# Q's parity copies by DMA, twenty more B1 blocks inside attention, and the second norm's apply on GpSimd

## The chip, the cores and the metric

The kernel runs on one core of a Trainium2 chip. The metric is the device time in microseconds (us) of one execution, the median of several runs. The engines are named as in the profile: PE is TensorE (PEld its weight loads), DVE is VectorE, ACT is ScalarE, POOL is GpSimd, SP is SyncE, which here issues every DMA.

## The reference

One block of a transformer with conditioning, in bf16, with S = 2048 tokens, D = 512 features, 32 heads of 16, a window of 256 keys, and F = 1792.

```python
mod = (silu(c) @ w_mod).reshape(1, 6, 1, 512)       # sa, ca, ga, sb, cb, gb
h = layernorm(x) * (1 + ca) + sa
x = x + ga * A(h)      # q, k, v = h @ wqkv; softmax over the last 256 keys; @ wo
h = layernorm(x) * (1 + cb) + sb
x = x + gb * B(h)

def B(x):              # a token-mixing MLP: it contracts over the 2048 tokens
    h = layernorm(x)
    u = gelu(einsum('bsd,sf->bdf', h, w1) + b1)     # "B1"
    y = einsum('bdf,fs->bds', u, w2) + b2           # "B2"
    return y.transpose(0, 2, 1)
```

Between the two halves each token thus passes a second norm with a scale and a shift (its result is called h2 in the kernel) and a third norm without them (its result is hb, the input of B1).

## The kernel before, in words

Tokens are worked in 16 blocks of 128 (`tb`, also `sc` where B1 contracts over them) and in 4 groups of 4 blocks (`tg`). Heads are worked in 4 groups of 8 (`g8`). Everything between startup and the tail is one stage, called attention here, whose order is written out by hand under `tc.manual_schedule()`: what is emitted first on an engine runs first on it.

**Units.** Attention is a loop over 80 units (`units`): 4 token groups x 4 head groups x 5 kinds (`KINDS`). Each unit has its scores on PE into PSUM (`emit_scores`, L548, L555, L575, L585), two exponentials of 128x1024 on ACT (`emit_exp`, L598), and its products with V on PE (`av_a` L609, `av_c` L623). After units 2 and 4 of a head group the product leaves PSUM by a transpose on DVE (`norm_out`, L655). When both have left, `norm_rest` divides: a reciprocal on DVE (L666), a multiply on POOL that writes `merge` (L667), and a transpose back on DVE that writes `OTd` (L675).

**Dense groups.** Each unit can also carry one dense group: four times four matmuls of 128x32 columns (`dense`, L271) into the single PSUM tile `dn`, and its eviction on DVE. `plan` lays out which: the projections Q, K and V of this token group and of the next (`qk_group`, `v_group`), the transposes of the next group's normalised tokens (`transpose_group`, L253), the output projection `wo_group` of the previous group's tokens (its eviction, L370, adds to x), and, in the last group, `part_group`: B1 blocks for the columns `fc` in `PART`, over the token blocks that are ready, accumulated in PSUM and kept as `part` in SBUF. A tail loop starts those columns at `sc` = 8. Groups 1 and 2 have a dense group in all units but 16 and 19, group 3 in all but 11.

**Q by parity.** Scores of even and of odd heads use the same rows of K, so Q is kept twice, `QT[:, 0]` with the odd heads' rows at zero and `QT[:, 1]` with the even heads' rows at zero. `qk_group` evicts Q to `qs` on DVE (L309), and POOL multiplies it by the two masks (L313).

**Second and third norm.** `ln23` follows each output projection in three steps: p1 takes statistics of x (DVE L683 and L685; then POOL L204 and L208 for one over the root), p2 applies them on DVE (L695) and scales and shifts on POOL (L699, L700), p3 takes statistics of h2 and applies them on POOL (L214 and L215, `apply_by_pool`) into `hb`. These steps, the divisions and the first norm of the next group wait in lists (`chains`); `fill` emits a step when a planner's clock of DVE and POOL says that there is room. So the planned costs set the order on DVE and POOL. At most LIVE = 4 token blocks are between p2 and p3.

**DMAs.** SP issues them in order. In attention these are `copies_for` (L633: the pieces of V for the unit kind "C", for the first head group at unit 0, for the others at units 3, 4 and 5), and in group 1 the first NA = 10 of 16 blocks of w1, half a block a unit, each paced behind an exponential (L408). The other blocks of w1 (`w1b`) and w2 are loaded when attention has ended.

**Tail.** PE runs B1 for the columns 0 to 5 over `sc` 0 and 1, then the output projection of the last four blocks (`t_wo`, L986, which reads all four `OTd[3]`), interleaved with `sc` 2 and 3; then `sc` 4 to 15 (L964); then the other columns in pairs (L1050), their gelu (`emit_gelu`, which first adds `part` on DVE, L973, for the columns that have it), and B2 (L1086) with its result.

Of the kernel before, what the change touches and what calls it, by code (L numbers as in the profile page):

```python
# [8 lines left out]
DT = mybir.dt  # L9
ACT = mybir.ActivationFunctionType  # L10
ALU = mybir.AluOpType
# [10 lines left out]
NF = F // P  # L22
EPS = 1e-5
SCORE_SCALE = DH ** -0.5
NA = 10
LIVE = 4
SLACK = 0.3

# [2 lines left out]
def kernel(  # L31
# [59 lines left out]
    hbpool = ctx.enter_context(tc.tile_pool(name="hbpool", bufs=1))  # L91
    hb = [hbpool.tile([P, D], DT.bfloat16, name=f"hb_{t}") for t in range(NT)]
    opool = ctx.enter_context(tc.tile_pool(name="opool", bufs=2))

    PART = (6, 7, 8, 9)
    ppool = ctx.enter_context(tc.tile_pool(name="ppool", bufs=1))
    part = {fc: ppool.tile([P, D], DT.float32, name=f"part{fc}") for fc in PART}
    wqpool = tc.alloc_tile_pool(name="wqpool", bufs=1)
# [66 lines left out]
    build_masks()  # L165


    qpool = tc.alloc_tile_pool(name="qpool", bufs=2)
    kpool = tc.alloc_tile_pool(name="kpool", bufs=1)
    vpool = tc.alloc_tile_pool(name="vpool", bufs=1)  # L170
    qspool = tc.alloc_tile_pool(name="qspool", bufs=2)
# [21 lines left out]
    nc.gpsimd.memset(ones[:], 1.0)  # L193


    for tg in range(NG):
        VaugT[tg] = Vring[tg % 2]
        for g8 in range(ND):
            KT[tg][g8] = Kring[tg % 2][:, g8, :]

# [91 lines left out]
    def qk_group(tg, g8, kind, pool):  # L292
        col0 = g8 * P + (D if kind == "k" else 0)

        def mms():
            pq = pool.tile([P, 4 * P], DT.float32, name="dn")
            for dc in range(ND):
                dense(
                    pq, lhsT=wqkv[:, dc, col0 : col0 + P], rhs=h1T[tg][:, dc, :],
                    start=(dc == 0), stop=(dc == ND - 1),  # L300
                )
            return pq

        def evac(pq):
            if kind == "k":
                nc.vector.tensor_copy(out=KT[tg][g8], in_=pq[:])  # L306
                return
            qs = qspool.tile([P, 4 * P], DT.bfloat16, name="qs")
            nc.vector.tensor_copy(out=qs[:], in_=pq[:])  # L309
            QT[tg][g8] = qpool.tile([P, 2, 4 * P], DT.bfloat16, name=f"QT{g8}")  # L310
            for n, m in enumerate((mask_even, mask_odd)):
                eng = nc.vector if (tg, g8, n) == (0, 1, 0) else nc.gpsimd
                eng.tensor_scalar(  # L313
                    out=QT[tg][g8][:, n, :], in0=qs[:], scalar1=m[:], scalar2=0.0, op0=ALU.mult, op1=ALU.add,
                )
            return 0.7 if (tg, g8) == (0, 1) else 1.4
        return mms, evac, (1.05 if (tg, g8, kind) == (0, 1, "q") else 0.7)
# [70 lines left out]
    with tc.manual_schedule():  # L388
# [116 lines left out]
        for dc in (0, 2, 1, 3):  # L505
            for ps, col0 in ((pq, 0), (pk, D)):
# [1 line left out]
                    ps, lhsT=wqkv[:, dc, col0 : col0 + P], rhs=h1T[0][:, dc, :],  # L508
                    start=(dc == 0), stop=(dc == ND - 1),
                )  # L510
        QT[0][0] = qpool.tile([P, 2, 4 * P], DT.bfloat16, name="QT0")

        def q_half(n, m, lo, hi):
            nc.vector.tensor_scalar(
# [145 lines left out]
        def norm_rest(tg, g8):  # L660
            t2v = state["t2"][:].rearrange("p a (b c) -> p a b c", c=32)
            m = npool.tile([P, 4 * P], DT.bfloat16, name="merge")

            def quotient():
                zr = npool.tile([P, 2, 16, 1], DT.float32, name="zr")
                nc.vector.reciprocal(out=zr[:], in_=t2v[:, :, :, DH : DH + 1])  # L666
                nc.gpsimd.tensor_tensor(  # L667
                    out=m[:].rearrange("p (b a d) -> p a b d", a=2, d=DH), in0=t2v[:, :, :, 0:DH],
                    in1=zr[:].to_broadcast([P, 2, 16, DH]), op=ALU.mult,
                )  # L670
                return 1.06

            def back():
                OTd[tg][g8] = opool.tile([P, 4 * P], DT.bfloat16, name=f"OTd{g8}")
                nc.vector.transpose(out=OTd[tg][g8][:], in_=m[:])  # L675
            return [(quotient, 0.36), (back, 0.72)]

        def ln23(tb):
            v = {}

            def stats(src, key):
                st = small.tile([P, nc.vector.BN_STATS_DIM], DT.float32, name="ln2_stats")
                nc.vector.bn_stats(out=st[:], in_=src)  # L683
                v[key] = small.tile([P, nc.vector.BN_AGGR_DIM], DT.float32, name="ln2_mv")
                nc.vector.bn_aggr(out=v[key][:], in_=st[:])  # L685
                v[key + "r"] = rstd_of(v[key][:, 1:2], 1, "ln2")

            def p1():
                stats(xres[tb][:], "m2")
                return 0.85  # L690

            def p2():
                live.add(tb)
                h2 = v["h2"] = lnpool.tile([P, D], DT.bfloat16, name="h2")
                nc.vector.tensor_scalar(  # L695
                    out=h2[:], in0=xres[tb][:], scalar1=v["m2"][:, 0:1], scalar2=v["m2r"][:],
                    op0=ALU.subtract, op1=ALU.mult,
                )
                nc.gpsimd.tensor_tensor(out=h2[:], in0=h2[:], in1=bc_cb1, op=ALU.mult)  # L699
                nc.gpsimd.tensor_tensor(out=h2[:], in0=h2[:], in1=bc_sb, op=ALU.add)  # L700
                return 2.4

            def p3():
                stats(v["h2"][:], "m3")
                apply_by_pool(hb[tb][:], v["h2"][:], v["m3"][:, 0:1], v["m3r"][:])
                done.add(tb)
                live.discard(tb)
                return 2.0
            return [(p1, 0.8), (p2, 0.37, lambda: len(live) < LIVE), (p3, 0.8)]

        chains = []
        live = set()
# [25 lines left out]


        def part_group(fc, k):  # L740
            def mms():
                assert done >= set(range(4 * k, 4 * k + 4))
                if k == 0:
                    part[fc, "ps"] = ps_dn.tile([P, D], DT.float32, name="dn")
                for sc in range(4 * k, 4 * k + 4):
                    dense(
                        part[fc, "ps"], lhsT=w1box["a"][:, sc, fc * P : (fc + 1) * P], rhs=hb[sc][:],
                        start=(sc == 0), stop=(sc == 7),
                    )
                return part[fc, "ps"]  # L750

            def evac(ps):
                if k == 1:
                    nc.vector.tensor_copy(out=part[fc][:], in_=ps[:])
            return mms, evac, 0.7 * k


        wo_next = iter(range(12))
# [1 line left out]
        def plan(tg):  # L760
            at, then = {}, {}

            def lay(ul, group):
                assert ul not in at, (tg, ul)
                at[ul] = group

            def qk(ul, g, g8, kind):
                lay(ul, qk_group(g, g8, kind, ps_dn))

            for n in (2, 3):  # L770
                lay(n - 2, v_group(tg, n, ps_dn))
            if tg == 0:
                for ul, g8, kind in ((2, 1, "q"), (3, 1, "k"), (4, 2, "q"), (5, 2, "k"), (6, 3, "q"), (7, 3, "k")):
                    qk(ul, tg, g8, kind)
                lay(8, bias_group(ps_dn))
                lay(13, bc_group(ps_dn))
                then[18] = [(lambda g=g: fold_wod(g), 0.0) for g in range(ND)]
            else:
                for ul, g8, kind in ((2, 1, "k"), (3, 2, "q"), (4, 2, "k"), (5, 3, "q"), (8, 3, "k")):
                    qk(ul, tg, g8, kind)  # L780
                for ul in (6, 7, 9, 10):
                    tb = next(wo_next)
                    lay(ul, wo_group(tb, ps_dn))
                    then[ul] = ln23(tb)
            if tg + 1 < NG:
                t0, t1, q0, v0, k0, q1, v1 = (10, 11, 12, 16, 14, 15, 18) if tg == 0 else (11, 12, 13, 14, 15, 17, 18)
                lay(t0, transpose_group(tg + 1, 0, ps_dn))
                lay(t1, transpose_group(tg + 1, 1, ps_dn))
                lay(v0, v_group(tg + 1, 0, ps_dn))
                lay(v1, v_group(tg + 1, 1, ps_dn))  # L790
                for ul, g8, kind in ((q0, 0, "q"), (k0, 0, "k"), (q1, 1, "q")):
                    qk(ul, tg + 1, g8, kind)
            else:
                for n, fc in enumerate(PART):
                    for k in range(2):
                        lay(12 + 2 * n + k, part_group(fc, k))
            return at, then
# [235 lines left out]
    with tc.tile_pool(name="gtmp", bufs=2) as gtmp:  # L1033
# [9 lines left out]
        for n, fg in enumerate(fgroups[2:]):  # L1043
            pu = ps_u[n % 2].tile([P, 2, D], DT.float32, name=f"pu{n % 2}")
            for sc in range(NT):
                for i, fc in enumerate(fg):
                    s0 = 8 if fc in PART else 0
                    if sc < s0:
                        continue
                    nc.tensor.matmul(  # L1050
                        pu[:, i, :], lhsT=w1_of(sc, fc), rhs=hb[sc][:],
                        start=(sc == s0), stop=(sc == NT - 1),
                    )
            for i, fc in enumerate(fg):
                emit_gelu(pu, i, fc, gtmp)
# [67 lines left out]
```

## Time and profile before

| what | value |
|---|---|
| runs | 267.12, 264.77, 265.92 us; median 265.92 |
| profiled execution | 264.77 us, of which the span from first to last instruction is 263.0 |
| granted TensorE clock, mean | 0.993 |
| PE busy | 240.8 us (92%) |
| DVE busy | 167.2 us (64%) |
| ACT busy | 164.3 us (62%) |
| POOL busy | 128.6 us (49%) |
| first and last exponential start | 13.6 and 164.2 us |
| chain that ended last | PE 70%, DVE 18%, ACT 5%, issue 3%, DMA 2% |

The shares are averages over three stages: startup to 13.6 us, attention to about 166 us, and the tail. In attention PE, ACT, DVE and POOL all work; in the tail it is PE, with DVE and ACT for gelu and the result. A line of a group reads: source line, engine, operation, out<-in with shapes, count, then busy us and mean ns of one, then the idle time of its engine before it and what ended that.

### The profile page before, as it was taken

What the parts mean: (1) busy time and instruction counts of PE and PEld (TensorE: products, weight loads), DVE (VectorE), ACT (ScalarE), POOL (GpSimd) and SP (SyncE); (2) the same over time, 40 slices, a digit from 0 to 9 for tenths busy, and PEclk for the clock granted to TensorE, in tenths of its full rate; (3) what the DMA queues carried; (4) which work ended last, traced back from release to release, by engine and by line L of the source; (5) the groups of instructions that cost most, each with busy time, mean ns of one, the idle gap of its engine ahead of it and who ended that gap; (6) DMA issues with size and microseconds to landing.
All of it is one profiled execution on the core that took longest, in us unless ns stands there. A gap on an engine that the chain in (4) does not pass through costs nothing.

```text
span 263.0 us, 11079 instructions
## 1 busy us (share of the span) xinstructions
PE 240.8 (92%) x4923; PEld 129.6 (49%) x4933; DVE 167.2 (64%) x353; ACT 164.3 (62%) x193; POOL 128.6 (49%) x218
## 2 busy tenths in 40 slices
PE   6988798899998879989899899999999999999994
PEld 2544455455555545555456455444444444444443
DVE  6678868875798697898786877789411001423444
ACT  6688998999999989999999999100082110000000
POOL 6104943699269998898995498954200000000000
PEclk9999979999999999999999999999999999999999
DMA  5949962134744342000122000999800000202021
GB/s 168 340 143 250 245 215 79 47 89 123 224 130 133 110 129 73 6 2 5 32 75 53 5 2 24 333 417 414 356 3 0 2 0 0 80 2 80 20 101 40
DMA packets 26084, 29.95 MB, mean 114 GB/s; under 512 B 3252, under 2 KB 23476, under 8 KB 26036
## 3 DMA queue, kind: packets, MB, share of 16 engines
q1 hardware_dynamic: 26036, 29.25, 35.4%
q8 instruction: 38, 0.62, 1.0%
q14 instruction: 10, 0.08, 0.1%
HBM read 22.55 MB, written 2.23 MB: 94 GB/s over the span
## 4 chain that ended last, share of the span: by engine, by line
PE 70%; DVE 18%; ACT 5%; issue 3%; DMA 2%; SPq 1%; ACTq 0%; DVEq 0%
PE dn L271 19%; PE py L1086 18%; PE pu L1050 8%; PE pu L964 7%; PE pss L548 5%; ACT et L598 5%; PE po L609 4%; PE po L623 3%; DVE t L655 3%; DVE qs L309 3%; DVE VaugT L287 2%; DMA wmod<-in_w_mod_dram 2%; PE pss L555 2%; DVE KT L306 2%; DVE x L370 1%
## 5 line engine op out<-in xcount | busy, mean ns | idle before, releaser
L598 ACT ACTIVATE et<-pss 128x1024 bf16<-128x1024 f32 (+1 forms) x160 | 143.8, 995 | 6.4 <-PE pss L555 5.1
L1086 PE MATMUL py<-guT,w2r 128*128 128x512 bf16 (+1 forms) x234 | 48.3, 366 | 0.2
L1065 DVE SCALAR_TENSOR_TENSOR o<-py,bFM,bc 128x512 bf16<-128x512 f32 (+1 forms) x17 | 11.7, 715 | 44.4 <-PE py L1086 44.4
L271 PE MATMUL dn<-h1T,wqkv 128*32 128x512 bf16 x496 | 33.1, 381 | 3.9 <-DVE VaugT L287 1.3
L1086 PEld LDWEIGHTS <-w2r 128*128 128x128 bf16 x238 | 23.3, 98 | 25.3
L548 PE MATMUL pss<-QT,KT 32*128 32x64 bf16 (+2 forms) x704 | 28.9, 238 | 5.8 <-ACT et L598 4.8
L655 DVE STREAM_TRANSPOSE t<-po 128x512 f32<-128x512 f32 x32 | 22.8, 711 | 11.4 <-PE po L623 11.2
L208 POOL TENSOR_TENSOR ln_rstd<-ln_ve,mhalf 128x1 f32<-128x1 f32 (+1 forms) x40 | 24.1, 602 | 5.7 <-DVE ln_ve L204 2.6
L204 POOL TENSOR_SCALAR ln_ve<-ln_mv 128x1 f32<-128x1 f32 (+1 forms) x38 | 9.1, 240 | 34.7 <-DVE ln_mv L226 17.6
L548 PEld LDWEIGHTS <-KT 32*128 32x128 bf16 x704 | 15.4, 92 | 21.3 <-issue 11.1
L609 PE MATMUL po<-et,VaugT 128*32 128x64 bf16 (+2 forms) x704 | 25.1, 241 | 0.0
L609 PEld LDWEIGHTS <-VaugT 128*32 128x32 bf16 x704 | 17.2, 96 | 11.0 <-issue 2.1
L271 PEld LDWEIGHTS <-wqkv 128*32 128x32 bf16 x512 | 13.1, 95 | 13.5 <-issue 6.0
L555 PE MATMUL pss<-mask_q,mask_k 32*128 32x256 bf16 (+1 forms) x256 | 19.2, 263 | 0.0
L667 POOL TENSOR_TENSOR merge<-t,zr 128x512 bf16<-128x512 f32 x16 | 17.0, 1060 | 3.2 <-DVE zr L666 3.2
L271 PE MATMUL dn<-wqkv,h1T 128*32 128x512 bf16 x240 | 15.7, 380 | 2.2 <-DVE VaugT L287 1.2
L975 ACT ACT_TABLE_LOAD x1 | 1.3, 1283 | 24.9 <-PE pu L964 24.9
L699 POOL TENSOR_TENSOR h<-h,bc 128x512 bf16<-128x512 bf16 x12 | 14.0, 1166 | 3.5 <-DVE h L695 3.5
L271 PE MATMUL dn<-wod,OTd 128*32 128x512 bf16 x192 | 12.6, 381 | 2.0 <-DVE KT L306 1.0
L700 POOL TENSOR_TENSOR h<-h,bc 128x512 bf16<-128x512 bf16 x12 | 13.9, 1155 | 0.9
L964 PE MATMUL pu<-hb,w1a 128*128 128x512 bf16 x58 | 13.2, 379 | 0.2 <-issue 0.2
L623 PE MATMUL po<-et,Vc 128*32 128x64 bf16 x960 | 13.0, 194 | 0.0
(113 smaller groups left out, 363.7 us busy)
## 6 DMA issues: line engine op xcount, KB each, us to landing
w2r<-in_B_w_dram SPq DMA_DIRECT2D x14, 512.0 KB, 10.1
w1a<-in_B_w_dram SPq DMA_DIRECT2D x20, 224.0 KB, 3.3
w1b<-in_B_w_dram SPq DMA_DIRECT2D x6, 448.0 KB, 7.5
Vc<-VaugT SPq DMA_DIRECT2D x32, 64.0 KB, 2.3
wmod<-in_w_mod_dram SPq DMA_DIRECT2D x8, 256.0 KB, 5.1
out_dram<-otile SPq DMA_DIRECT2D x15, 128.0 KB, 1.7
x<-in_A_x_dram SPq DMA_DIRECT2D x6, 256.0 KB, 4.2
Vc<-VaugT SPq DMA_DIRECT2D x12, 128.0 KB, 3.6
```

Source lines behind the costliest of these rows:

```text
L208: nc.gpsimd.tensor_tensor(out=r[:], in0=ve[:], in1=mhalf[:, 0:n], op=ALU.pow)
L271: nc.tensor.matmul(out[cols, :], lhsT=lhsT[:, cols], rhs=rhs, start=start, stop=stop, tile_position=(0, 32 * j), skip_group_check=True,)
L548: nc.tensor.matmul(pss[j // 2][:, j % 2, c0 : c0 + nq], lhsT=keys(kb, g8)[rows[j], k0 : k0 + P], rhs=QT[tg][g8][rows[j], par, q0 : q0 + nq ...
L555: nc.tensor.matmul(pss[j // 2][:, j % 2, :].rearrange("p (a r) -> p a r", a=2)[:, 0:n, :] .rearrange("p a (b q) -> p a b q", q=64)[:, :, 0 ...
L598: act = nc.scalar.activation(out=et[:, :, 0:n], in_=state.pop((u, a))[:, :, 0:n], func=ACT.Exp, scale=SCORE_SCALE,)
L609: nc.tensor.matmul(state["po"][32 * j : 32 * j + 32, q0 : q0 + nq], lhsT=VaugT[kb // 4][:, kb % 4, 8 * g8 + 2 * j + par, :], rhs=state["e" ...
L623: nc.tensor.matmul(state["po"][32 * j : 32 * j + 32, q0 : q0 + 64], lhsT=Vc[half][:, b, 8 * g8 + 2 * j + par, :], rhs=state["e", tg, g8, 2 ...
L655: nc.vector.transpose(out=state["t2"][:, par, :], in_=state["po"][:])
L667: nc.gpsimd.tensor_tensor(out=m[:].rearrange("p (b a d) -> p a b d", a=2, d=DH), in0=t2v[:, :, :, 0:DH], in1=zr[:].to_broadcast([P, 2, 16, ...
L964: nc.tensor.matmul(pu[:, i, :], lhsT=w1_of(sc, fc), rhs=hb[sc][:], start=(sc == 0), stop=(sc == NT - 1),)
L1050: nc.tensor.matmul(pu[:, i, :], lhsT=w1_of(sc, fc), rhs=hb[sc][:], start=(sc == s0), stop=(sc == NT - 1),)
L1086: nc.tensor.matmul(pys[n][:, 0 : hi - lo], lhsT=w2r[:, fc, tb * P : (tb + 1) * P], rhs=guT[fc][:, lo:hi], start=(fc == 0), stop=(fc == NF ...
```

## The change

Three things change. Q of token groups 2 and 3 is no longer masked on POOL: eight DMAs of 16 rows copy its heads from `qs` into the half of their parity, over the tiles of groups 0 and 1, whose other rows are zero already. `PART` grows from four columns of B1 with 8 token blocks to five with 8 and three with 4, which makes 52 blocks instead of 32; the dense groups that this needs stand in the units that had none, and some projections move to earlier units. And `ln23` has two steps: the apply of the second norm moves from DVE to POOL, in one step with its statistics. To make room in SBUF, only NA = 8 blocks of w1 are loaded in attention, and two of the four `OTd` tiles have one buffer.

```diff
-NA = 10
+NA = 8
...
+    opool1 = ctx.enter_context(tc.tile_pool(name="opool1", bufs=1))
-    PART = (6, 7, 8, 9)
+    PART = {6: 8, 7: 8, 8: 8, 9: 8, 10: 4, 11: 4, 12: 8, 13: 4}
...
-    qpool = tc.alloc_tile_pool(name="qpool", bufs=2)
+    qpool = tc.alloc_tile_pool(name="qpool", bufs=1)
...
+    Qring = [[qpool.tile([P, 2, 4 * P], DT.bfloat16, name=f"QT{r}{g8}") for g8 in range(ND)] for r in range(2)]
     for tg in range(NG):
+        for g8 in range(ND):
+            QT[tg][g8] = Qring[tg % 2][g8]
...
             nc.vector.tensor_copy(out=qs[:], in_=pq[:])
-            QT[tg][g8] = qpool.tile([P, 2, 4 * P], DT.bfloat16, name=f"QT{g8}")
+            if tg >= 2:
+                for row in range(0, P, DH):
+                    head = slice(row, row + DH)
+                    dma.dma_start(out=QT[tg][g8][head, row // DH % 2, :], in_=qs[head, :])
+                return
             for n, m in enumerate((mask_even, mask_odd)):
...
             def p1():
                 stats(xres[tb][:], "m2")
-                return 0.85
-
-            def p2():
                 live.add(tb)
                 h2 = v["h2"] = lnpool.tile([P, D], DT.bfloat16, name="h2")
-                nc.vector.tensor_scalar(
-                    out=h2[:], in0=xres[tb][:], scalar1=v["m2"][:, 0:1], scalar2=v["m2r"][:],
-                    op0=ALU.subtract, op1=ALU.mult,
-                )
+                apply_by_pool(h2[:], xres[tb][:], v["m2"][:, 0:1], v["m2r"][:])
                 nc.gpsimd.tensor_tensor(out=h2[:], in0=h2[:], in1=bc_cb1, op=ALU.mult)
                 nc.gpsimd.tensor_tensor(out=h2[:], in0=h2[:], in1=bc_sb, op=ALU.add)
-                return 2.4
+                return 4.3
...
-            return [(p1, 0.8), (p2, 0.37, lambda: len(live) < LIVE), (p3, 0.8)]
+            return [(p1, 0.9, lambda: len(live) < LIVE), (p3, 0.9)]
...
         def part_group(fc, k):
+            last = k == PART[fc] // 4 - 1
...
-                        start=(sc == 0), stop=(sc == 7),
+                        start=(sc == 0), stop=(sc == PART[fc] - 1),
...
-                if k == 1:
+                if last:
                     nc.vector.tensor_copy(out=part[fc][:], in_=ps[:])
-            return mms, evac, 0.7 * k
+            return mms, evac, 0.7 * last
...
-                for ul, g8, kind in ((2, 1, "k"), (3, 2, "q"), (4, 2, "k"), (5, 3, "q"), (8, 3, "k")):
+                if tg == 1:
+                    order = ((2, 1, "k"), (3, 2, "q"), (4, 2, "k"), (5, 3, "q"), (8, 3, "k"))
+                else:
+                    order = ((2, 2, "k"), (3, 3, "q"), (4, 3, "k"))
+                for ul, g8, kind in order:
                     qk(ul, tg, g8, kind)
-                for ul in (6, 7, 9, 10):
+                for ul, fc, k in {2: ((8, 10, 0), (10, 11, 0)), 3: ((8, 13, 0), (10, 12, 0), (11, 12, 1))}.get(tg, ()):
+                    lay(ul, part_group(fc, k))
+                for ul in (6, 7, 9, 10) if tg == 1 else (5, 6, 7, 9):
                     tb = next(wo_next)
                     lay(ul, wo_group(tb, ps_dn))
                     then[ul] = ln23(tb)
...
+                if tg:
+                    qk(16, tg + 1, 1, "k")
+                    qk(19, tg + 1, 2, "q")
...
-                    s0 = 8 if fc in PART else 0
+                    s0 = PART.get(fc, 0)
```

More of the change, by code (lines that the diff above doesn't have):

```diff
@@ L510 @@
                 )
-        QT[0][0] = qpool.tile([P, 2, 4 * P], DT.bfloat16, name="QT0")
         def q_half(n, m, lo, hi):
@@ L673, in back @@
             def back():
-                OTd[tg][g8] = opool.tile([P, 4 * P], DT.bfloat16, name=f"OTd{g8}")
+                OTd[tg][g8] = (opool if g8 < 2 else opool1).tile([P, 4 * P], DT.bfloat16, name=f"OTd{g8}")
                 nc.vector.transpose(out=OTd[tg][g8][:], in_=m[:])
@@ L792, in plan @@
                     qk(ul, tg + 1, g8, kind)
+                if tg:
+                    qk(16, tg + 1, 1, "k")
+                    qk(19, tg + 1, 2, "q")
             else:
-                for n, fc in enumerate(PART):
+                for n, fc in enumerate((6, 7, 8, 9)):
                     for k in range(2):
```

## The prediction

> **What bounds the kernel now.** I read the page's slices first, then the groups, the waits of the attention stage, the chain, and last the order of time around its end.
>
> ```profile
> PE   6988798899998879989899899999999999999994
> ACT  6688998999999989999999999100082110000000
> POOL 6104943699269998898995498954200000000000
> PEclk9999979999999999999999999999999999999999
> ```
>
> A digit is 6.6 us. ACT is full until slice 25 (165 us): attention. Behind it only PE is full, to the end: B1 and B2. POOL is near full from slice 10 on and stops about one slice after ACT. So attention is shared by ACT, PE and POOL, and the tail is PE's alone. Two lines of the waits between 53 and 168 us, and of the order of time, show how close:
>
> ```profile
> PE pss L548 <- ACT et L598: 2.7, 5, 0.6
> 95.02 1.05 PE L271 MATMUL dn<-h1T,wqkv 128*32 128x512 bf16 x16 [0.94 <-DVE VaugT L287]
> 93.17 1.20 DVE L695 TENSOR_SCALAR h<-x,ln_mv,ln_rstd 128x512 bf16<-128x512 bf16 x1
> ```
>
> In three token groups PE waits for ACT only 2.7 us, at the five units that have no dense group: that is all the room PE has. The second line is PE's longest wait there, 0.94 us, behind an L695 that took 1.20 us instead of its usual 0.41.
>
> Costs of single instructions (busy, mean ns):
>
> ```profile
> L215 POOL TENSOR_SCALAR hb<-h,ln_rstd,shift 128x512 bf16<-128x512 bf16 x12 | 9.1, 762 | 1.3
> L214 POOL TENSOR_SCALAR shift<-ln_mv,ln_rstd 128x1 f32<-128x1 f32 x24 | 6.4, 265 | 1.5
> L695 DVE TENSOR_SCALAR h<-x,ln_mv,ln_rstd 128x512 bf16<-128x512 bf16 x12 | 6.3, 540 | 0.1
> L313 POOL TENSOR_SCALAR QT<-qs,mask_even 128x512 bf16<-128x512 bf16 x14 | 9.7, 692 | 5.9 <-DVE qs L309 5.9
> ```
>
> And POOL and the chain where attention ends:
>
> ```profile
> 166.29 1.15 POOL L700 TENSOR_TENSOR h<-h,bc 128x512 bf16<-128x512 bf16 x1
> 167.40 1.05 POOL L667 TENSOR_TENSOR merge<-t,zr 128x512 bf16<-128x512 f32 x1
> 168.54 0.23 POOL L204 TENSOR_SCALAR ln_ve<-ln_mv 128x1 f32<-128x1 f32 x1
> 170.72 0.23 POOL L204 TENSOR_SCALAR ln_ve<-ln_mv 128x1 f32<-128x1 f32 x1
> ...
> 168.71 0.61 DVE OTd L675
> 169.36 1.25 PE pa L986 x5
> ...
> 198.94 10.74 PE pu L1050 x49
> ```
>
> The last merge starts the moment POOL is free (its reciprocal ended at 167.15), OTd follows, and t_wo(12) uses it at 169.36. Before that PE runs 12 B1 matmuls of sc 0 and 1 from 166.12, so PE waits under 0.2 us. POOL is thus just in time here. This is the place I price most carefully.
>
> **The change, part by part.**
>
> *Tail.* 20 of 128x128 blocks leave the B1 loop. 49 matmuls take 10.74 us, 0.219 each: 20 x 0.219 = **-4.4 us**. Four more adds (L973, 0.69 us) lie on DVE, idle there; guT[12] and [13] are first used 48 B2 matmuls (10.5 us) after B1 ends. w1b grows by two loads of 448 KB, but sc 8 is used some 15 us after attention. I take nothing for these.
>
> *PE in attention.* Five more dense groups of 1.0 us start to start (units 16 and 19 of groups 1 and 2, unit 11 of group 3) fill exactly the five units with PE's waits: 5.0 - 2.7 = +2.3 us. Against it, L695 leaves DVE, and with it the 0.94 us wait at 95.02. Net **+1.4 us**. DVE gets 4 more evictions (0.68 each) and loses 12 applies (6.3 us); that it gets emptier I count at nothing more.
>
> *POOL.* The second norm's apply adds 12 x (0.265 + 0.762 and two gaps of 0.1), about 1.2 us a block. First step (p1) by start times: ve to next start in a statistics-and-apply step is 170.72 - 168.54 = 2.18; the two tensor_tensor add 1.24 + 1.2, less an overlap: 4.54 us. Second step (p3) stays 2.18. Away go 16 mask products, 11 us, all in groups 1 to 3. The sum for POOL hardly moves (+3 us), but the mask products leave from early units and the applies arrive at the end, where POOL is just in time. The order of POOL's queue in the changed kernel shows it: in group 3, from token block 7's p1 on, stand p1(7), merge, p1(8), p3(7), merge, p3(8), p1(9), p1(10), p1(11), merge, p3(9), p3(10), and only then the last merge. That is 5 x 4.54 + 4 x 2.18 + 4 x 1.04 = 35.6 us without a gap. The statistics of block 7 follow Q's eviction of unit 3, which ends now at 136.8; plus 0.9 for them, 137.6. With no shift of the units the last merge would end at 173.3 and OTd at about 174; before it ended at 169.3.
>
> The same queue delays group 2. By the same durations from 70.67 on, p3(3) ends at 108.6, while unit 8's new group wants hb_3 at about 107.5: 1.0 us. The last xn1 ends at 114.2, wanted by the transposes of unit 11 at 113.7: 0.5 us. So the units of group 3 are late by 1.0 (two groups' fills less the 0.94) + 1.5 = 2.6 us at unit 3, and with them p1(7): OTd ends at 176.5, against 169.3: **+7.2 us** for t_wo, the +1.4 of PE and the 1.5 included. PE has 2.6 us of sc 0 and 1 after attention ends at about 169 and then stands still for about 5 us.
>
> *Q's copies.* Each of 8 Q groups issues 8 DMAs of 16 KB on SP. The nearest issues take 0.36 to 0.44 us:
>
> ```profile
> 1.64 0.42 SPq L116
> ...
> 88.31 2.87 SPq L633 DMA_DIRECT2D Vc<-VaugT  x3
> ...
> Vc<-VaugT SPq DMA_DIRECT2D x32, 64.0 KB, 2.3
> ```
>
> 8 x 0.42 = 3.4 us, and 2.3 to land. Q itself is wanted 6 to 11 units (1.9 us each) after its eviction: hidden. Queued behind the copies of unit 19 are the three Vc copies of the next group's first heads. They now start at 88.31; then at about 93.6, and land 2 + 2.1 us later at 97.7. The products of unit 2 want them at 96.9 (96.7 now). That is 0.8 us in groups 2 and 3 each; the bounds are 0 (SP's issue at 0.36 with no hiccup) and 2 (one of its issues of 1.5 us). As POOL is later still, I take nothing on the path.
>
> *Clock.* PE's idle of 5 us may cost more than itself. In this run one stretch had half clock, after PE was 68% busy for 3.3 us:
>
> ```profile
> 31.00:34.30 3.30, 2.24 (x70) 1.44 (x67) 2.32 (x7) 3.23 (x5) 3.01 (x7) 1.00 1.01 287
> 34.30:37.70 3.40, 3.36 (x66) 1.92 (x63) 2.43 (x6) 3.00 (x4) 1.90 (x3) 0.50 0.85 272
> ```
>
> Columns: stretch, length, busy PE, PEld, DVE, ACT, POOL, then granted clock, DMA. A stretch of 3.4 us at half clock costs 0 (inside the idle) to 1.7 us; I take 0.4. [...]
>
> **Sum.** -4.4 + 7.2 + 0.4 = **+3.2 us**. The profiled execution took 264.77 (span 263.0, 1.8 around it): 268.0. It is the fastest of the three, 1.15 below their median 265.92; on the median, **269.1 us**. Unknown terms: shift of the units 0 to 3.5 us, POOL's chain 1 us either way, clock 0 to 1.7, giving 266.5 to 272 for this case.
>
> [...] The row is 762 ns in all 24 cases of L215, and the row decides.
>
> **Rivals.**
> *POOL is not late* (faster). If the last merge comes within 2.6 us of attention's end, the B1 matmuls of sc 0 and 1 cover it, and only PE counts: -4.4 + 1.4 = -3.0, or -1.5 with group 2's waits: 262.9 to 264.4 on the median. It decides when the 35.6 us of queue shrink under about 31, so that p1 costs under 3.7 us. For it: POOL has 6 us of gaps in slices 21 and 22 (138 to 147). Against: in the profile now, POOL runs gapless from 147.29 to 168.45, and each of its long rows there is within 0.05 us of its mean.
> *SP's queue decides* (slower still). If an issue of a Q copy takes 0.6 as Vc's do, unit 19's copies take 4.8 us, unit 3's delay the Vc copies of heads 8 to 15 too, and each of groups 2 and 3 loses 1.5 to 2 us more: 272.5. For it: 64 issues are added to a queue where some took 1.5. Against: 16 rows are fewer than the 64 of Vc.
> *The copies do not relieve POOL.* It is part of the first sum: the masks that go were in the early units.
>
> **How the numbers follow.** Chances: forecast 0.55; POOL not late 0.27; SP's queue 0.12; anything outside 0.06. A measurement of this kernel can tell about 1%, 2.7 us, from no change. The forecast's spread puts 0.43 above 268.6 and 0.12 within 1%; the fast rival lies across 263.3, 0.14 below and 0.13 within; SP's queue is all above; of the rest 0.04 is below and 0.02 above. Faster 0.18, same 0.25, slower 0.57. The range runs from the fast rival's end, 262.8, to the slow one's, 272.8.
>
> **What would show it.** Right: POOL gapless through group 3's last 30 us; a wait of PE pa for OTd of 4 to 6 us near 172 to 177; the last merge starting 4 us or more after its reciprocal; B1's second loop 4.4 us shorter; attention's last exponential 1.5 to 3.5 us later. Wrong: t_wo right behind sc 1 (first rival), or PE waiting for DMA Vc in groups 2 and 3 (second). If the apply on POOL takes well under 0.76 us, or POOL's blocks 9 to 11 start earlier than 153 us, the step that fails is the 35.6.

## The result and the profile after

The changed kernel takes **290.63 us** (median of four runs, 288.64 to 290.94); the kernel before took 265.37 in the same comparison. The ratio is 1.0924, with a 95% interval of 1.085 to 1.0999. The profiled execution took 290.94 us with a span of 289.2, which is 26.2 more than the 263.0 of before.

The slices of the page, now 7.2 us a digit:

```profile
PE   6788779899988449798947889967999999999995
ACT  7488998999999608799972979900004521000000
POOL 5105936693884925847821868886430000000000
PEclk9999999999999958999995999995999999999999
```

In before, attention had no hole: ACT read 9 nearly throughout and the clock was 9 almost throughout. Now PE and the clock drop together at three places: slices 14 to 16 and 21 to 22, where ACT falls too, and 27 to 28, the end of attention. The waits between 53 and 200 us name the cause of the first two, then of the third (columns: total, times, longest):

```profile
PE po L634 <- DMA Vc<-VaugT: 16.5, 7, 6.4
...
PE pa L1002 <- DVE OTd L686: 5.0, 1, 5.0
```

Neither stood in the waits of before. The first is a stand for pieces of V that SP had not yet sent, in groups 2 and 3. SP's own order of time shows why:

```profile
87.99 6.09 SPq L321 DMA_DIRECT2D QT<-qs  x8
94.18 1.07 SPq L420 DMA_DIRECT2D w1a<-in_B_w_dram  x1
95.36 6.11 SPq L321 DMA_DIRECT2D QT<-qs  x8
101.57 2.04 SPq L644 DMA_DIRECT2D Vc<-VaugT  x3
```

The second column is the time that the issues took. Eight copies of Q take 6.1 us, so the eight of unit 17 and the eight of unit 19 stand back to back. The first three V copies of the group, issued from 88.31 in the kernel before, come at 101.57. PE meanwhile:

```profile
97.05 0.28 PE L566 MATMUL pss<-mask_q,mask_k 32*128 32x256 bf16 x4
103.72 0.25 PE L634 MATMUL po<-et,Vc 128*32 128x64 bf16 x4 [6.40 <-DMA Vc<-VaugT]
105.11 0.56 PE L634 MATMUL po<-et,Vc 128*32 128x64 bf16 x28 [1.14 <-DMA Vc<-VaugT]
```

PE stops at 97.33 and stands 6.40 us. The granted clock falls at 100.6 and stays at half for 10.2 us; two stretches by windows (after the length: PE, PEld, DVE, ACT, POOL busy, then the clock):

```profile
105.10:110.80 5.70, 5.65 (x100) 2.63 (x104) 2.86 (x5) 1.94 (x2) 1.48 (x4) 0.50 0.03 9
110.80:116.00 5.20, 4.79 (x173) 2.90 (x165) 3.79 (x9) 4.57 (x5) 3.08 (x6) 1.00 0.15 37
```

In the first, PE is busy for nearly all of the 5.7 us and gets through 100 matmuls; in the 5.2 us of the second it gets through 173. The trace has three such stretches, from 100.6 (10.2 us), 151.8 (6.8) and 196.1 (6.8), each begun within a stand of PE. 16.2 us of PE's busy time lie in them, at a granted clock of 0.50, so about 8.1 us are lost. Before had one stretch, which cost about 1.7 (half of the 3.36 us that PE was busy in it).

The end of attention went as forecast in its order and its lengths, though some 20 us later. POOL's last merge and the rows ahead of it:

```profile
180.91 0.23 POOL L211 TENSOR_SCALAR ln_ve<-ln_mv 128x1 f32<-128x1 f32 x1
185.57 0.23 POOL L211 TENSOR_SCALAR ln_ve<-ln_mv 128x1 f32<-128x1 f32 x1
...
190.10 1.06 POOL L678 TENSOR_TENSOR merge<-t,zr 128x512 bf16<-128x512 f32 x1
...
195.49 1.05 POOL L678 TENSOR_TENSOR merge<-t,zr 128x512 bf16<-128x512 f32 x1
```

One p1 is 185.57 - 180.91 = 4.66 us. OTd follows the last merge at 196.58 and t_wo runs at 197.35 after the 5.0 us stand.

The 26.2 us of span, put together:

| part | us |
|---|---|
| PE waits for Vc, groups 2 and 3 | +16.5 |
| PE waits for OTd at the end | +5.0 |
| half clock, less that of before (worked out) | +6.4 |
| 20 B1 blocks less in the tail (from the run with the blocks alone) | -4.5 |
| rest: denser attention about 2.0, startup 1.15 (first exponential 14.79 against 13.64) | +2.8 |

The last row is what remains; the two pieces named for it make 3.15 when they are measured by themselves. The startup part is a wait for a modulation weight that landed late, 6.17 us behind its issue against 5.03 in before. It does not come with the change: in the changed kernel with Q masked on POOL, whose startup is the same, the first exponential starts at 13.55.

### The profile page after: what moved, and what is told of

Same layout as the page of the kernel before. It is cut to its first block, busy times and chain, and to the rows that moved or that the text cites. A ratio compares the mean times of both kernels' runs of the same rounds, so it can differ in the third digit from the quotient of the medians.

```text
span 289.2 us, 11301 instructions
## 1 busy us (share of the span) xinstructions
PE 245.7 (85%) x4993; PEld 130.7 (45%) x4993; DVE 167.1 (58%) x349; ACT 165.4 (57%) x193; POOL 130.6 (45%) x226
## 4 chain that ended last, share of the span: by engine, by line
PE 55%; DVE 13%; POOL 12%; SPq 6%; DMA 5%; issue 4%; ACT 3%; ACTq 0%; DVEq 0%; POOLq 0%
PE py L1102 17%; PE dn L278 13%; PE pu L980 7%; PE pu L1066 6%; SPq L321 3%; DMA Vc<-VaugT 3%; PE pss L559 3%; PE po L620 3%; ACT et L609 3%; POOL h L704 2%; POOL h L705 2%; PE po L634 2%; DVE t L666 2%; DMA wmod<-in_w_mod_dram 2%; POOL merge L678 2%
## 5 line engine op out<-in xcount | busy, mean ns | idle before, releaser
L278 PE MATMUL dn<-h1T,wqkv 128*32 128x512 bf16 x496 | 36.3, 411 | 4.4 <-DVE VaugT L294 1.4
L559 PE MATMUL pss<-QT,KT 32*128 32x64 bf16 (+2 forms) x704 | 26.8, 242 | 3.0 <-ACT et L609 2.2
L634 PE MATMUL po<-et,Vc 128*32 128x64 bf16 x960 | 14.1, 197 | 16.5 <-DMA Vc<-VaugT 16.5
L620 PEld LDWEIGHTS <-VaugT 128*32 128x32 bf16 x704 | 18.1, 97 | 11.8 <-issue 2.2
L559 PEld LDWEIGHTS <-KT 32*128 32x128 bf16 x704 | 14.3, 93 | 18.0 <-issue 9.7
L278 PEld LDWEIGHTS <-wqkv 128*32 128x32 bf16 x512 | 13.9, 100 | 16.2 <-issue 9.0
L634 PEld LDWEIGHTS <-Vc 128*32 128x32 bf16 x960 | 10.2, 98 | 19.3 <-DMA Vc<-VaugT 17.6
L989 DVE TENSOR_TENSOR gelu_a<-pu,part 128x512 f32<-128x512 f32 x8 | 5.2, 687 | 18.5 <-PE pu L1066 18.5
L1066 PE MATMUL pu<-hb,w1b 128*128 128x512 bf16 x64 | 14.3, 379 | 0.0
```

Source lines behind the costliest of these rows:

```text
L278: nc.tensor.matmul(out[cols, :], lhsT=lhsT[:, cols], rhs=rhs, start=start, stop=stop, tile_position=(0, 32 * j), skip_group_check=True,)
L559: nc.tensor.matmul(pss[j // 2][:, j % 2, c0 : c0 + nq], lhsT=keys(kb, g8)[rows[j], k0 : k0 + P], rhs=QT[tg][g8][rows[j], par, q0 : q0 + nq ...
L620: nc.tensor.matmul(state["po"][32 * j : 32 * j + 32, q0 : q0 + nq], lhsT=VaugT[kb // 4][:, kb % 4, 8 * g8 + 2 * j + par, :], rhs=state["e" ...
L634: nc.tensor.matmul(state["po"][32 * j : 32 * j + 32, q0 : q0 + 64], lhsT=Vc[half][:, b, 8 * g8 + 2 * j + par, :], rhs=state["e", tg, g8, 2 ...
L1066: nc.tensor.matmul(pu[:, i, :], lhsT=w1_of(sc, fc), rhs=hb[sc][:], start=(sc == s0), stop=(sc == NT - 1),)
```

## The experiments

All times below are medians, each compared with the kernel before on its own chip. Waits and half clock are from the profiled execution of each; for Q's copies alone and for both mends that execution is the longest of its runs, for POOL's apply alone the shortest.

| kernel | us | ratio, 95% interval | Vc waits | OTd waits | half-clock stretches, us |
|---|---|---|---|---|---|
| changed | 290.63 | 1.0924 [1.085, 1.0999] | 16.5 | 5.0 | 10.2, 6.8, 6.8 |
| blocks alone | 262.55 | 0.9872 [0.9845, 0.9899] | 0 | 0 | 3.4 |
| Q's copies alone | 275.17 | 1.0321 [1.0238, 1.0404] | 7.6 | 0 | 3.4, 3.4 |
| POOL's apply alone | 278.44 | 1.0458 [1.0391, 1.0525] | 0 | 3.6 | 3.4 |
| changed, Q masked on POOL | 275.48 | 1.0375 [1.0339, 1.041] | 0 | 5.4 | 3.4, 6.8 |
| changed, apply on DVE | 285.52 | 1.0718 [1.0661, 1.0775] | 18.9 | 0 | 3.4, 6.8, 3.4, 6.8, 3.4 |
| changed, 128 copies | 332.77 | 1.2526 [1.2446, 1.2606] | 45.6 | 5.0 | 71.7 in all |
| changed, 32 copies | 276.57 | 1.041 [1.0341, 1.0479] | 5.7 | 5.0 | 3.4, 6.8 |
| changed, Q later in SP's queue | 275.18 | 1.0324 [1.027, 1.0378] | 5.1 | 5.0 | 3.4, 3.4 |
| changed, last four blocks on DVE | 284.91 | 1.0718 [1.0658, 1.0778] | 17.9 | 0 | 3.4, 10.2, 3.4, 6.8 |
| Q masked on POOL, last four on DVE | 269.29 | 1.014 [1.0072, 1.0208] | 0 | 0 | 6.8 |
| Q later, last four on DVE | 267.59 | 1.0052 [1.0013, 1.0091] | 5.2 | 0 | 3.4, 3.4 |

The theory after the result: SP's issue time decides, since the Q copies delay the V copies; the apply on POOL adds its 5 us at the end; the clock follows both. The rivals: the transfers themselves (bytes) are late; or POOL alone is the cause and SP's wait only shows it.

### Taking one part back

**Q masked on POOL again**, all else as changed, and the planner told nothing of the masks, so that its order stays:

```diff
-            if tg >= 2:
+            if tg >= NG:
...
-            return 0.7 if (tg, g8) == (0, 1) else 1.4
+            return 0.7 if (tg, g8) == (0, 1) else 1.4 if tg < 2 else None
```

> The changed kernel with Q of groups 2 and 3 masked on GpSimd again; the order on all other engines stays as changed. Theory (SP's queue holds up the V copies, PE stands still, and its clock halves): no wait of PE for Vc, so 16.5 us of waits and some 5 us of half clock go, while GpSimd gets back 11 us of masks and is later at the end of attention than the 5.0 us of now (5 to 9 us): 268 to 274 us. Rival (the five more dense groups crowd attention, the copies only show it): above 282 us.

275.48 us, 1.5 above the upper end. Not one wait for Vc is left, so the copies cause them all, and without them the kernel is 290.63 - 275.48 = 15.2 us faster. What was not expected is a wait in group 2:

```profile
PE dn L278 <- POOL hb L222: 2.9, 1, 2.9
```

Ahead of this hb, POOL works from 89.17 to 110.90 without a gap, and 2.7 us of that are four mask products that the changed kernel doesn't have. So the wait belongs to the masks that were put back, together with the apply on POOL: none of the kernels with the copies shows it, nor do the blocks alone, with the masks but not the apply.

**The apply back on DVE**, as three steps with their old planned costs:

```diff
-            return [(p1, 0.9, lambda: len(live) < LIVE), (p3, 0.9)]
+            return [(p1, 0.8), (p2, 0.37, lambda: len(live) < LIVE), (p3, 0.8)]
```

> The changed kernel with the second norm applied by VectorE in three steps as before. Theory: SP's queue is the same, so PE still waits 14 to 17 us for Vc; the wait of the output projection for OTd falls from 5.0 to under 1 us: 283 to 287 us. Rival (GpSimd's queue is what delays attention): below 275 us.

285.52 us, as expected. The OTd wait is gone and the Vc waits are not:

```profile
PE po L634 <- DMA Vc<-VaugT: 18.9, 8, 6.6
```

So POOL is not behind SP's waits, and the rival that has POOL as the only cause falls.

### One part alone

**The 20 blocks alone**: both of the edits above.

> Only the 20 more B1 blocks: masks on GpSimd, second norm on VectorE. Theory, by the prediction's terms: -4.4 us in the tail, +1.4 in attention, no wait for Vc: 261 to 264 us. Rival (the added dense groups themselves cost some 10 us of attention): above 270 us.

262.55 us: this part is a gain of 1.3% (1.0 to 1.55), and this kernel is faster than both others. Its tail, from the first output projection to B2, takes 37.99 us where before took 42.53: -4.5. Attention, from first to last exponential, takes 2.0 us more.

**Q's copies alone** (the kernel before with the fixed Q tiles and the loop of copies, without the planner's new places for the projections):

> The kernel before with nothing changed but Q's copies by DMA in groups 2 and 3 (at its old units: head group 1 at unit 17, 2 at unit 3, 3 at unit 5). Theory: only one Q group (5.6 us of SP) stands ahead of the V copies of unit 0 and of unit 3, so PE waits 1 to 3 us for Vc at each, in two groups: 268 to 275 us, and no gain from the 11 us that GpSimd saves, since no wait ends with it but the last merge. Rival (freeing GpSimd pays): below 265 us.

275.17 us, at the upper edge of the range (the four runs lie from 271.96 to 276.52). The copies cost 10 us here, but 285.52 - 262.55 = 23.0 on top of the blocks. What differs is the order: here only one Q group stands ahead of the first V copies, which come at 96.53. The blocks' new plan moved another Q projection to unit 19, and with it eight more issues ahead of them.

**POOL's apply alone** (the kernel before with the two-step list, planned at 3.3 instead of 4.3 us):

```diff
-                return 2.4
+                return 3.3
...
-            return [(p1, 0.8), (p2, 0.37, lambda: len(live) < LIVE), (p3, 0.8)]
+            return [(p1, 0.9, lambda: len(live) < LIVE), (p3, 0.9)]
```

> The kernel before with nothing changed but the second norm's apply on GpSimd, in one step with its statistics (planned at 3.3 us in place of 4.3, since with the masks still there the planner has no room for 4.3). Theory (GpSimd has 14 us more to do and is just in time already): the last merge is late by 4 to 8 us, and hb or xn1 by some more in group 2 or 3: 269 to 277 us. Rival (VectorE gets emptier and attention shorter): below 265 us.

278.44 us, 1.4 above the range. The profiled execution took 275.58 and lies within it; the other three took 278.43 to 278.50, at a mean granted clock of 0.981 to 0.982 against its 0.994. Over 277 us that is some 7 us more of half clock, which is enough for the 2.9 us between them if PE is busy in it; these three left no trace to see it in. Here POOL keeps its 16 late masks and gets the applies, and PE waits for it at two places:

```profile
PE pa L980 <- DVE OTd L675: 3.6, 1, 3.6
PE dn L253 <- POOL xn L215: 2.8, 1, 2.8
```

### Is it the issue or the bytes?

**Each copy cut in two**, 128 issues of 8 KB instead of 64 of 16 KB, the same bytes:

```diff
-                    dma.dma_start(out=QT[tg][g8][head, row // DH % 2, :], in_=qs[head, :])
+                    for half in (slice(0, 2 * P), slice(2 * P, 4 * P)):
+                        dma.dma_start(out=QT[tg][g8][head, row // DH % 2, half], in_=qs[head, half])
```

> The changed kernel with every Q copy split in two by columns: 128 issues of 8 KB in place of 64 of 16 KB, the same bytes. Theory (the number of issues on SP, 0.6 to 0.7 us each whatever the size, sets when the V copies start): each Q group costs SP 11 us instead of 5.6, the first V copies of groups 2 and 3 start about 11 us later, PE's waits for Vc grow from 16.5 to over 40 us: 315 to 335 us. Rival (bytes or landing decide): within 5 us of 290.

332.77 us. PE now waits 45.6 us for V, and 6.4 us for Q itself, which it did not wait for with 64 copies:

```profile
PE po L635 <- DMA Vc<-VaugT: 45.6, 8, 16.2
PE pss L560 <- DMA QT<-qs: 6.4, 2, 3.2
```

**Half the copies**: the even heads by DMA, the odd ones by one mask on POOL:

```diff
-                for row in range(0, P, DH):
+                for row in range(0, P, 2 * DH):
                     head = slice(row, row + DH)
-                    dma.dma_start(out=QT[tg][g8][head, row // DH % 2, :], in_=qs[head, :])
+                    dma.dma_start(out=QT[tg][g8][head, 0, :], in_=qs[head, :])
+                nc.gpsimd.tensor_scalar(out=QT[tg][g8][:, 1, :], in0=qs[:], scalar1=mask_odd[:], ...)
```

> The changed kernel with only the even heads of Q copied by DMA (32 issues); the odd half is masked by GpSimd, 0.69 us each. Theory (number of issues): the first V copies of group 2 start about 6 us earlier, waits of PE for Vc fall from 16.5 to 2 to 6 us; GpSimd has 5.5 us more, so its waits stay at 5 to 6: 273 to 279 us. Rival (landing of any copy ahead decides): above 284 us.

276.57 us. With 32, 64 and 128 issues PE's waits for Vc are 5.7, 16.5 and 45.6 us. The rows of the issues (ns: least, median, most; then first and last start), of before, of the changed kernel and of the 128 copies:

```profile
L633 SPq DMA_DIRECT2D Vc<-VaugT x44: 590/597/1761, 15.4 to 139.1; - x44
```

```profile
L321 SPq DMA_DIRECT2D QT<-qs x64: 507/587/1768, 79.9 to 162.5; - x64
```

```profile
L322 SPq DMA_DIRECT2D QT<-qs x128: 507/587/1622, 79.5 to 203.2; - x128
```

Copies of 8, 16 and (V) 64 or 128 KB all have a median of 0.59 to 0.60 us. The same bytes in twice the issues nearly triple the wait, so it is the issue that costs, and the rival of the bytes falls.

### Mending each place

**Q's copies of head groups 2 and 3 later in SP's queue**, behind the V copies of units 0 and 5, and still ahead of their use:

```diff
                 copies_for(tg, max(ul - 2, 0))
+            if tg >= 2 and ul in (0, 5):
+                q_copies.pop((tg, 2 if ul == 0 else 3))()
```

> The changed kernel with Q's copies moved in SP's queue: those of head group 2 behind the three V copies of unit 0, those of head group 3 behind the last V copies of unit 5. Same number of copies. Theory (what is ahead of the V copies in the queue decides): waits of PE for Vc fall from 16.5 to under 4 us, the OTd wait stays near 5: 269 to 276 us. Rival (the sum of issues on SP decides, in whatever order): above 284 us.

275.18 us: 15 us of the 25 come back by an order alone, with the same 64 issues. Vc waits of 5.1 us remain, more than the 4 expected:

```profile
90.04 5.93 SPq L323 DMA_DIRECT2D QT<-qs  x8
96.07 1.18 SPq L426 DMA_DIRECT2D w1a<-in_B_w_dram  x1
97.34 2.04 SPq L650 DMA_DIRECT2D Vc<-VaugT  x3
```

One Q group and a load still stand ahead of the V copies, which come at 97.34 instead of 101.57. No wait for Vc is longer than 2.4 us now, and attention behind startup has no half clock until the stand at its end.

**The second norm of blocks 8 to 11 on DVE**, in the three old steps, the others as changed:

```diff
+            if tb >= 8:
+                return [(p1, 0.8), (p2, 0.37, lambda: len(live) < LIVE), (p3, 0.8)]
```

> The changed kernel with the second norm of the last four blocks that attention handles (8 to 11) applied by VectorE in three steps; blocks 0 to 7 stay on GpSimd. Theory (three first steps on GpSimd ahead of the last merge make the 5.0 us wait for OTd): that wait falls to under 1 us and the half-clock stretch behind it goes, waits for Vc stay at 15 to 18 us: 282 to 285.5 us. Rival (the end on GpSimd is hidden by what SP does): above 288 us.

284.91 us, as expected. The OTd wait goes and the Vc waits stay:

```profile
PE po L634 <- DMA Vc<-VaugT: 17.9, 7, 6.3
```

**The masks on POOL and the last four blocks on DVE:**

> The changed kernel with Q masked on GpSimd and the second norm of blocks 8 to 11 on VectorE. Theory: from 275.5 the wait for OTd of 5.4 us and its half-clock stretch go, the 2.9 us wait for hb in group 2 stays: 266 to 270.5 us. Rival (GpSimd is late everywhere with the masks): above 273 us.

269.29 us: without SP's and without POOL's late end, the hb wait of 2.8 us in group 2 and its 6.8 us of half clock are still there.

**Both mends in one kernel:**

> Both mends together: Q's copies behind the V copies in SP's queue, and the last four blocks' second norm on VectorE. If the two terms add up: 275.2 less 5.0 and some 1 us of half clock, 267.5 to 270.5 us, with about 5 us of waits for Vc left. Rival (one of the waits takes the other's place): above 273 us.

267.59 us, at the lower end of the range and 0.5% above before (0.1 to 0.9). Two changes of order and place thus recover nearly all of the 25 us. Against the masks on POOL (1.014) the copies in their later place look about 1% better, but the two intervals overlap. The blocks alone, at 0.9872, are the best of all.

## Why the prediction was wrong

The direction was right, and the size was not: 269.1 was forecast, with 272.8 as the upper end, and 290.63 was measured. By its own steps:

**Q's copies: wrong, and the main cause.** The failed step is "The nearest issues take 0.36 to 0.44 us", and after it "I take nothing on the path". Those rows are loads from DRAM. The row of the same kind, from SBUF to SBUF, was V's: 0.597 us in the median, and 2.87 us for three in the line shown right below. The copies took 0.587 in the median and 0.695 in the mean, since 8 of them in a row take 5.9 to 6.1 us, not 3.4. On the path they made 16.5 us of waits for Vc instead of nothing; PE waiting for Vc in groups 2 and 3 is the sign that the prediction itself named for its second rival. The argument against the rival, that "16 rows are fewer than the 64 of Vc", is refuted: an issue of 16 KB took 0.587 us in the median, one of V's 64 or 128 KB 0.597. The rival itself had the right mechanism and 12 in 100, but a price of 1.5 to 2 us a group; measured were 9.4 in group 2 and 7.1 in group 3. It let unit 19's copies delay V and forgot unit 17's ahead of them: at 3.4 us a group these end with unit 19's eviction (91.34), at 6.1 they end at 94.08. The V copies were forecast at 93.6 and came at 101.57. Of these 8.0 us, 2.7 are that carry-over, 2.7 the longer issues of unit 19's own copies, 1.4 a load of w1 between the two with the gaps, and 1.1 the later eviction, about as much as startup was late.

**The clock: wrong.** 0.4 us was taken, for one stand of 5 us. There were three stretches at half clock, worth about 6.4 us net. The three falls come 3.2, 3.7 and 3.8 us after PE stopped. The first stretch then lasted 10.2 us, where the term was worked out from the one of 3.4 us in before. The stand at the end alone brought 6.8 us with 5.55 us of PE's busy time in them: 2.8 us instead of 0.4.

**POOL's queue at the end: right.** The order came as listed, from p1(7) at 157.94 to the last merge at 195.49. To the end of that merge it is 38.6 us with 2.6 us of waits in it, so 36.0 of work against 35.6 forecast; p1 4.66 against 4.54, the apply 0.762 as taken, the stand 5.0 us against "about 5 us". The wait is 5.0 in the changed kernel, with 32 copies, with 128 and with Q later: it moves with the units, as worked out, and has nothing to do with SP. "POOL gapless" was not quite so, by those 2.6 us; nor was it in before, where two waits for DVE, of 0.5 and 0.3 us, lie between 147.29 and 168.45.

**POOL's queue in group 2: not shown.** None of the kernels with the copies has a wait for hb_3 or xn1. Their units are late there by the waits for Vc, which could cover the 1.0 and 0.5 us, so this term stays open. The 2.9 us with the masks on POOL are not this term, since four mask products of 2.7 us stand ahead of them. That kernel's 275.48 is therefore not the forecast with SP's miss taken out. Of its 10.1 us of added span the OTd waits have 5.4, the hb wait 2.9, the half clock 3.7 (7.38 us of PE's busy time in it) less the 1.7 of before, and the waits for the eviction of K on DVE 2.3 (3.3 against 1.0); the blocks take off 4.5 and denser attention adds 2.0.

**Tail and fill: right.** -4.4 was forecast and -4.5 measured; +1.4 for the five dense groups, and 2.0 of longer attention with the blocks alone. PE's waits for ACT shrank from 4.8 us to 2.2 over the whole span, as the five units were filled. Blocks alone came at 262.55, 3.6 us under before; the terms for it gave 3.0.

**The rival of POOL not late** is refuted by the 5.0 us. "The copies do not relieve POOL" holds: at the end POOL is as late with the copies (5.0) as with the masks (5.4).

What stays open: why some issues, 9 of the 64, take 1.0 to 1.8 us instead of 0.59; and what decides whether half clock follows a stand, which no run varied by itself. The price of the clock is worked out from the records and was not separated by a run. Fewer and larger copies, one DMA over several heads' rows, and copies issued by another engine than SP were not run.

## What to carry to other kernels

Price a DMA that is added to a queue by its issues, not its bytes (here 0.587 us at 8 KB as at 16, and 0.597 at V's 64 and 128), and by the row with the same source and destination; then write out the queue in order and let each group start where the one ahead of it ends, because a group that fits its slot at 3.4 us pushes the next one at 6.1. Before work is moved to a queue, list what stands behind it and who waits for that: here three V copies, 2 us of SP's time, decided when PE could go on. And where PE is made to stand, price the half clock that may follow along with the stand: in the changed kernel, where it began within stands of 4.35 to 6.40 us, it came to about a quarter of the loss, by the working above.

## What the hardware showed that was not expected

- An issue on SP from SBUF to SBUF took 0.587 us in the median for 8 KB and for 16 KB, and 0.597 for V's 64 and 128 KB; a load of w1 from DRAM took 0.382 in the same queue (the changed kernel, 16 loads of 224 KB).
- The stretches of half clock had lengths of 3.4 us in before, and of 10.2, 6.8 and 6.8 in the changed kernel; with 128 copies they were 71.7 us in all, at a mean clock of 0.89.
- The length of a stand alone didn't decide. One of 3.08 us was followed by a stretch (Q's copies alone, where the next dense group of 16 matmuls took 1.92 us, against 1.05 ahead of the stand), one of 3.6 us by none (POOL's apply alone, clock 1.00 during it and in the 6.8 us after it).
- Nor did half clock come only where PE had stood still: in before PE was busy for 2.24 of the 3.30 us ahead of its one stretch, from 31.0 to 34.3 us.
